# Weight transfers that also wait for the landing of the fourth one ahead

## The chip, the core and the metric

The kernel runs on one core of a Trainium2 chip. The metric is the device time of one execution in microseconds (us); the time before is the median of three runs. The core has a matrix engine (TensorE, PE; its weight loads are listed as PEld), a vector engine (VectorE, DVE), a scalar engine (ScalarE, ACT), GpSimd (POOL) and SyncE (SP). SP computes nothing here: it issues the transfers that bring weights from the chip's main memory to the core. The transfers run on 16 DMA engines, and the landing of a transfer is told to the other engines by a semaphore.

## The reference, cut to what matters

```python
x = A_x
x = x + _A_ref(_layernorm(x), A_mem0, A_Wq, A_Wk, A_Wv, A_Wo, 32)   # attention with a memory
x = x + _B_ref(_layernorm(x), B_w1, B_w2, B_w3, B_w4)               # mixer and MLP
x = x + _A_ref(_layernorm(x), A_mem0, A_Wq, A_Wk, A_Wv, A_Wo, 32)
x = x + _B_ref(_layernorm(x), B_w1, B_w2, B_w3, B_w4)

def _A_ref(x, mem0, Wq, Wk, Wv, Wo, seg_len):     # S = 2048, Dm = 640, 32 heads of 192, M = 8
    mem = mem0
    for s in range(S // seg_len):                 # 64 segments of 32 tokens, one after the other
        h = concatenate([mem, xs], axis=1)        # 40 rows
        q, k, v = h @ Wq, h @ Wk, h @ Wv          # each Wq, Wk, Wv: 640 x 6144
        o = softmax(mask(q @ k.T * scale)) @ v @ Wo
        mem = o[:, :M, :]                         # the next segment's memory
        outs.append(o[:, M:, :])
```

`_B_ref` is a gelu layer of 640 x 640 (`w1`), a shift of quarters of the channels along the tokens, a second layer of 640 x 640 (`w2`), and an MLP 640 to 1536 to 640 (`w3`, `w4`) with layer norms and residuals. All data is bf16. Each segment depends on the memory of the one before, so the 64 segments of an attention layer cannot be run together, and every segment needs all of the attention weights again.

## The kernel before

**Lanes and steps.** The work is cut into 69 steps, one call of `attention_step(t)` each. The first attention layer works on segment t in step t (lane 0), the second one on segment t - 5 (lane 1, `LAG` is 5). Steps 0 to 4 have lane 0 alone, steps 64 to 68 lane 1 alone, and the steps between have both lanes, whose 40 rows each are put side by side as 80 columns. In every second step the mixer and MLP of 64 tokens of each lane are worked in between (`chunk`, `chunk_end`).

**Weights.** They do not all fit on the core. Some stay (`wo` and parts of `wq`, `wk`, `wv`); the rest is brought again in every step. `load_pair` (L802) brings one row block of `Wq`, `Wk` or `Wv` for eight heads, 128 x 1536 values or 384 KB, into one of the 12 buffers of a ring (`wst`, `RING_A`). `load_b` (L838 to L844) brings a piece of `w1` to `w4`, 320 or 160 KB, into one of three buffers (`wstB`, `RING_B`). The projections on TensorE (`keys_queries`, L928, and `values3`, L984) use a block a few microseconds after it has landed. `project` (L1122) multiplies by the `wo` that stays; L1044 makes the scores, L1079 the transposes, L1096 the product with the values.

**Order.** All operations of all steps are handed to a planner (`Plan`) with a cost each, a due time (in steps of 48 us of its own reckoning) and the buffers they use. `place` lays them out in one list, and each engine executes its part in that order. For a weight transfer the planner reckons with a rate and with a lead (`DMA_AHEAD`) over its model of the transfers' line; where this moves a transfer later than its buffer would ask, it is marked `paced`, and the kernel ties it to the TensorE operation that the plan has ended by then:

```python
elif o.paced:
    k = len(done) - 1
    while k >= 0 and done[k].end + PE_LAT > o.start + PACE:
        k -= 1
    if k >= 0:
        tc.add_manual_dep(o.last, done[k].last.name, dep, reason="pace")
```

So SP issues the transfers in the list's order, each after its waits: for TensorE (the pacing, or the last use of the buffer), and for a landing. Eight semaphores tell of the landings of SP's transfers in turn, so a transfer also waits for the landing of the eighth one ahead of it, which used the same semaphore.

Of the kernel before, what the change touches and what calls it, by code (L numbers as in the profile page):

```python
# [20 lines left out]
LAG = 5  # L21
# [4 lines left out]
STEP = 48.0  # L26
# [35 lines left out]
RATE_ONE = 350.0e3  # L62
NSTEPS = 64
LAST_PACE = 0.55


RANK = {
# [517 lines left out]
def kernel(  # L585
# [707 lines left out]
    def chunk(c):  # L1293
        last = c == NCH - 1
        base = (T_A if last else 2 * c + 2) * STEP
        D = lambda x: base + (x * LAST_PACE if last else MIX[0] + x * MIX[1]) * STEP
        plan.at("last" if last else "chunk", base)
# [257 lines left out]
    def chunk_end(c):  # L1555
        last = c == NCH - 1
        base = (T_A if last else 2 * c + 2) * STEP
        D = lambda x: base + (x * LAST_PACE if last else MIX[0] + x * MIX[1]) * STEP
        plan.at("last_end" if last else "chunk_end", base)
# [125 lines left out]
    ctx.enter_context(tc.manual_schedule())  # L1685
    dep = mybir.DependencyInfo(mybir.DependencyClass.Sync, mybir.DependencyReason.DATA)
    done = []
    for o in placed:
        k = len(nc.cur_bb.bb.instructions)
        o.fn(o)  # L1690
        o.last = nc.cur_bb.bb.instructions[-1]
        for x in o.after:
            tc.add_manual_dep(nc.cur_bb.bb.instructions[k], x.last.name, dep, reason="after")
        if o.e == "PE":
            done.append(o)
        elif o.paced:
# [5 lines that stand above are left out]
# [35 lines left out]
```

## Time and profile before

| | us |
|---|---|
| time, median of three runs | 3266.26 (3263.81 to 3273.18) |
| the profiled execution's own time | 3268.68 |
| its span in the profile | 3266.9 |
| TensorE busy (PE) | 3149.0 |
| weight loads busy (PEld) | 2790.2 |
| VectorE / ScalarE / GpSimd busy | 2285.5 / 1854.6 / 269.6 |
| moved by DMA | 833.44 MB, 255 GB/s in the mean |
| granted TensorE clock | 0.993 of full speed |

A profile is one execution. PE and PEld overlap, so their sum means nothing. A row of waits says which engine stood idle before which line, and whose work or whose transfer ended that; "issue" means that no such cause is recorded. A "q" behind an engine's name (SPq) is its sequencer, which only waits and issues. The time "to landing" of a transfer runs from its issue on SP to the last of the 16 signals of its semaphore.

### The profile page before, as it was taken

The numbers are of one execution on the slowest core, as the hardware profiler recorded it, in microseconds if no ns is written. First come the engines' busy times: TensorE is split into PE (matmuls) and PEld (weight loads), VectorE is DVE, ScalarE is ACT, GpSimd is POOL, SyncE is SP. The second block draws the span as 40 slices with busy tenths as digits, with TensorE's granted clock in tenths as the row PEclk, the third lists the DMA queues.
The fourth block names the chain that finished last, engine by engine and source line by source line (L and its number), as shares of the span: only waits on it lengthen the run. The fifth ranks groups of instructions, "written<-read, shape, count | busy, mean of one in ns | idle before, by whom it ended". The sixth has DMA issues, their size and how long they took to land.

```text
span 3266.9 us, 172868 instructions
## 1 busy us (share of the span) xinstructions
PE 3149.0 (96%) x77161; PEld 2790.2 (85%) x77161; DVE 2285.5 (70%) x7377; ACT 1854.6 (57%) x4217; POOL 269.6 (8%) x510
## 2 busy tenths in 40 slices
PE   5899999999999999999999999999999999999997
PEld 4778888888888888888888888888888888888875
DVE  3566777777677777777777777777777777767665
ACT  2345565666556666656565666565656665556443
POOL 0000000000000000000000000000000000000000
PEclk8999999999999999999999999999999999999999
DMA  9787777778777877787777777777877787778885
GB/s 372 264 286 236 237 265 253 241 235 273 246 237 249 280 239 234 253 272 239 245 262 258 241 237 269 253 241 244 281 247 238 244 274 249 238 244 277 275 277 199
DMA packets 409714, 833.44 MB, mean 255 GB/s; under 512 B 39651, under 2 KB 207280, under 8 KB 408969
## 3 DMA queue, kind: packets, MB, share of 16 engines
q1 hardware_dynamic: 401704, 809.47, 73.2%
q0 software_dynamic: 7104, 12.84, 1.3%
q8 instruction: 604, 9.90, 1.2%
q14 instruction: 142, 1.16, 0.1%
q10 hardware_dynamic: 160, 0.08, 0.0%
HBM read 816.98 MB, written 5.24 MB: 252 GB/s over the span
## 4 chain that ended last, share of the span: by engine, by line
PE 88%; DMA 7%; issue 2%; DVE 2%; ACT 1%; SPq 0%; POOL 0%; POOLq 0%; ACTq 0%; DVEq 0%
PE psq L928 16%; PE psy L1122 16%; PE psk L928 16%; PE psv L984 15%; PE pss L1044 5%; PE pso L1096 5%; PE psh L1531 3%; DMA wst<-in_A_Wq_dram 3%; PE y L1577 3%; PE pst L1079 2%; DMA wst<-in_A_Wk_dram 2%; PE psv L1024 2%; PE psh L1409 1%; PE hs L1468 1%; DMA wst<-in_A_Wv_dram 1%
## 5 line engine op out<-in xcount | busy, mean ns | idle before, releaser
L928 PEld LDWEIGHTS <-wst 128*128 128x128 bf16 x19872 | 803.7, 99 | 64.1 <-issue 35.7
L1122 PE MATMUL psy<-oT,wo 128*128 128x80 bf16 (+1 forms) x16560 | 703.6, 200 | 26.4 <-issue 8.6
L964 ACT CAST V<-psv 96x384 bf16<-96x384 f32 (+3 forms) x1264 | 595.9, 474 | 168.3 <-PE psv L984 102.4
L1122 PEld LDWEIGHTS <-wo 128*128 128x128 bf16 x16560 | 630.8, 99 | 51.2 <-issue 35.1
L928 PE MATMUL psq<-hT,wst 128*128 128x80 bf16 (+1 forms) x9936 | 518.0, 200 | 13.7 <-DMA wst<-in_A_Wq_dram 8.6
L928 PE MATMUL psk<-hT,wst 128*128 128x80 bf16 (+1 forms) x9936 | 508.6, 200 | 17.7 <-DVE hT L1149 9.6
L939 ACT CAST qT<-psq 128x480 bf16<-128x480 f32 (+1 forms) x552 | 291.8, 529 | 371.2 <-PE psq L928 352.0
L1104 ACT CAST oT<-pso 128x480 bf16<-128x480 f32 (+1 forms) x552 | 293.7, 532 | 264.0 <-PE pso L1096 238.9
L954 DVE CAST kT<-psk 64x160 bf16<-64x160 f32 (+1 forms) x1104 | 340.4, 308 | 131.3 <-PE psk L928 62.6
L984 PEld LDWEIGHTS <-hT 128*32 128x32 bf16 (+1 forms) x11840 | 295.5, 96 | 157.0 <-issue 5.2
L1063 ACT ACTIVATE Pm<-pss,sm 80x320 bf16<-80x320 f32 (+2 forms) x552 | 279.3, 506 | 195.9 <-DVE sm L1056 105.2
L1056 DVE CUSTOM_DVE_ANT_1 pss<-pss,mask 80x320 f32<-80x320 f32 (+2 forms) x552 | 257.1, 466 | 150.1 <-PE pss L1044 138.3
L1087 ACT COPY PT<-pst 80x320 bf16<-80x320 bf16 (+2 forms) x552 | 221.7, 402 | 239.2 <-PE pst L1079 233.3
L984 PE MATMUL psv<-wst,hT 128*32 128x384 bf16 (+1 forms) x5920 | 343.3, 326 | 2.2 <-issue 1.1
L984 PE MATMUL psv<-wv,hT 128*32 128x384 bf16 x5920 | 344.7, 328 | 0.5 <-issue 0.5
L1067 DVE TENSOR_REDUCE sm<-Pm 80x4 f32<-80x320 bf16 (+2 forms) x552 | 250.5, 454 | 109.6 <-ACT Pm L1063 98.1
L928 PE MATMUL psq<-hT,wq 128*128 128x80 bf16 (+1 forms) x6624 | 321.1, 200 | 4.1 <-DMA wq<-in_A_Wq_dram 2.7
L928 PE MATMUL psk<-hT,wk 128*128 128x80 bf16 (+1 forms) x6624 | 321.0, 200 | 3.4 <-issue 2.0
L928 PEld LDWEIGHTS <-wk 128*128 128x128 bf16 x6624 | 270.8, 99 | 17.6 <-issue 13.9
L947 DVE CAST kT<-psk 128x320 bf16<-128x320 f32 (+1 forms) x552 | 253.8, 460 | 45.6 <-PE psk L928 33.5
L1069 DVE TENSOR_TENSOR Pm<-Pm,sm 80x320 bf16<-80x320 bf16 (+2 forms) x552 | 256.2, 464 | 34.9 <-DVE sm L1068 0.9
L928 PEld LDWEIGHTS <-wq 128*128 128x128 bf16 x6624 | 267.4, 99 | 6.5 <-DMA wq<-in_A_Wq_dram 3.0
(131 smaller groups left out, 3777.6 us busy)
## 6 DMA issues: line engine op xcount, KB each, us to landing
wst<-in_A_Wk_dram SPq DMA_DIRECT2D x556, 384.0 KB, 4.9
wst<-in_A_Wq_dram SPq DMA_DIRECT2D x556, 384.0 KB, 5.0
wst<-in_A_Wv_dram SPq DMA_DIRECT2D x418, 384.0 KB, 5.1
wstB<-in_B_w_dram SPq DMA_DIRECT2D x495, 320.0 KB, 4.7
wstB<-in_B_w_dram SPq DMA_DIRECT2D x132, 160.0 KB, 4.3
wo<-in_A_Wo_dram SPq DMA_DIRECT2D x8, 960.0 KB, 12.3
wv<-in_A_Wv_dram SPq DMA_DIRECT2D x2, 1536.0 KB
xw<-in_A_x_dram POOLq DMA_DIRECT2D x32, 77.5 KB, 5.3
```

Source lines behind the costliest of these rows:

```text
L928: nc.tensor.matmul(out=o[:, cc, 0:W], lhsT=wv(kc, GW * j + cc * P, GW * j + (cc + 1) * P), rhs=h[:, kc, cw:cw + W], start=begin(pq), stop= ...
L939: nc.scalar.copy(out=qT[:, :, c0:c0 + N], in_=T(pq)[:, :, off:off + N])
L947: nc.vector.tensor_copy(out=k4[:, :, 0::3, c0:c0 + N], in_=p4[:, :, 0::2, off:off + N])
L954: copy(out=k4[r0:r1, :, jj, c0:c0 + N], in_=p4[r0:r1, :, 1, off:off + N])
L964: (nc.vector.tensor_copy if e == "DVE" else nc.scalar.copy)(out=v_part(*dst), in_=a_)
L984: nc.tensor.matmul(out=o[32 * u:32 * u + n3, :], lhsT=left[:, kc, 32 * g3:32 * g3 + n3], rhs=wv(kc, a, a + GWH), start=(kc == 0), stop=(kc ...
L1056: nc.vector.tensor_tensor_reduce(out=o, in0=o, in1=maskt.unsqueeze(1).to_broadcast([NR, HG, N]), scale=-scale, scalar=3.0e38, op0=ALU.add, ...
L1063: nc.scalar.activation(out=Pb[0:NR, :, 0:N], in_=o, func=ACT.Exp, bias=sm_[0:NR, 0:1], scale=-1.0)
L1067: nc.vector.tensor_reduce(out=sm_[0:NR, 2:2 + HG], in_=Pb[0:NR, :, 0:N], axis=AX.X, op=ALU.add)
L1069: nc.vector.tensor_tensor(out=Pb[0:NR, :, 0:N], in0=Pb[0:NR, :, 0:N], in1=sm_[0:NR, 6:6 + HG].unsqueeze(2).to_broadcast([NR, HG, N]), op=A ...
L1104: nc.scalar.copy(out=o_[:, :, off:off + N], in_=T(pso)[:, :, 0:N])
L1122: nc.tensor.matmul(out=o[:, m, cw:cw + W], lhsT=wo[:, cc, m * P:(m + 1) * P], rhs=o_[:, cc, 0:W], start=st, stop=True, skip_group_check=True)
```

## The change

In steps with two lanes, which the change takes as those transfers of SP whose due time lies from step 5 to step 63, each transfer is given one more dependence: on the landing of the transfer that stands four places ahead of it among these. The dependence is added as the list is written out, after the planner is done; the plan, the order on every engine, the buffers and the pacing are as before.

```diff
+FLYING = 4
...
     done = []
+    flying = []
     for o in placed:
         k = len(nc.cur_bb.bb.instructions)
         o.fn(o)
         o.last = nc.cur_bb.bb.instructions[-1]
         for x in o.after:
             tc.add_manual_dep(nc.cur_bb.bb.instructions[k], x.last.name, dep, reason="after")
+        if o.e == "SP" and o.dma and LAG * STEP <= o.due < NSTEPS * STEP:
+            flying.append(o)
+            if len(flying) > FLYING:
+                tc.add_manual_dep(o.last, flying[-1 - FLYING].last.name, dep, reason="flying")
         if o.e == "PE":
             done.append(o)
```

## The prediction

> **What bounds the kernel now.** I read the page from the top (busy time, slices, chain), then the waits of TensorE, then the weight queue alone: its issues in order of time, the time to landing, and the busy share of the DMA engines by stretch.
>
> The page, sections 1, 2 and 4:
>
> ```profile
> span 3266.9 us, 172868 instructions
> PE 3149.0 (96%) x77161; PEld 2790.2 (85%) x77161; DVE 2285.5 (70%) x7377; ACT 1854.6 (57%) x4217; POOL 269.6 (8%) x510
> ...
> DMA  9787777778777877787777777777877787778885
> ...
> PE 88%; DMA 7%; issue 2%; DVE 2%; ACT 1%; SPq 0%; POOL 0%; POOLq 0%; ACTq 0%; DVEq 0%
> ```
>
> TensorE works 96% of the span and is 88% of the chain. So whatever delays its weights goes straight into the span, and the most that any change to the weights can win is what TensorE now loses to them. The waits of TensorE in the steps with two lanes (260 to 3070 us; columns: waited for, total us, times, longest us) say how little that is:
>
> ```profile
> PEld L928 <- issue: 37.8, 99, 1.1
> PEld L1044 <- issue: 28.9, 88, 1.2
> PEld L928 <- DMA wst<-in_A_Wq_dram: 10.8, 21, 1.2
> PEld L928 <- DMA wst<-in_A_Wk_dram: 5.7, 12, 0.9
> ```
>
> Waits on weights are 10.8 + 5.7 = 16.5 us of 2810 us, plus about 1 us on `wstB`. "Issue" is a wait for nothing that the profile shows; most are short.
>
> Now the weight queue (SP). First its issues around one burst (start, us, line, count):
>
> ```profile
> 1532.22 1.26 SPq L802 DMA_DIRECT2D wst<-in_A_Wk_dram  x2
> 1534.44 1.27 SPq L802 DMA_DIRECT2D wst<-in_A_Wq_dram  x2
> ...
> 1547.70 2.20 SPq L802 DMA_DIRECT2D wst<-in_A_Wk_dram  x3
> 1551.04 2.26 SPq L802 DMA_DIRECT2D wst<-in_A_Wq_dram  x3
> 1554.17 2.81 SPq L840 DMA_DIRECT2D wstB<-in_B_w_dram  x3
> ```
>
> Second the time from issue to landing (last column) at the burst's first two transfers, and between 1544 and 1558 us:
>
> ```profile
> wst<-in_A_Wk_dram SPq DMA_DIRECT2D x2, 384.0 KB, 3.4
> ...
> wst<-in_A_Wk_dram SPq DMA_DIRECT2D x4, 384.0 KB, 5.7
> wst<-in_A_Wq_dram SPq DMA_DIRECT2D x4, 384.0 KB, 5.6
> ```
>
> Third the stretches of one pair of steps (last columns: clock, DMA share, GB/s):
>
> ```profile
> 1532.00:1544.00 12.00, 12.00 (x306) 10.78 (x303) 9.71 (x33) 7.30 (x17) 2.12 (x3) 1.00 0.86 275
> 1544.00:1558.00 14.00, 14.00 (x341) 12.52 (x339) 10.32 (x33) 9.69 (x21) 0.44 (x2) 1.00 0.95 333
> 1566.00:1580.00 14.00, 13.95 (x348) 12.54 (x345) 9.67 (x32) 9.08 (x21) 0.00 (x0) 1.00 0.39 110
> 1580.00:1596.00 16.00, 16.00 (x389) 14.46 (x389) 12.07 (x37) 9.03 (x20) 0.00 (x0) 1.00 0.96 318
> ```
>
> The weights come in two bursts of some 32 us per pair of steps (94 us), with pauses between. In a burst the DMA engines are 95% busy, a transfer starts about every 1.07 us (28 from 1532.2 to 1562.2, counted in the timeline) and needs 5.6 us to land, against 3.2 to 3.4 us when nothing is ahead of it.
>
> **The change part by part.** Nothing is moved: in the two instruction lists all five engines have the same instructions in the same order. What differs is a wait at 1,857 of the 2,200 transfers on SP. Before, a transfer waits for the TensorE work that it is paced by and for the use of its buffer, and (as the completion semaphores go round in eight) for the landing of the eighth ahead. Now it waits for the fourth ahead. Four terms follow.
>
> (a) SP's own time. The wait is carried by a semaphore instruction that is there already; SP is idle most of the time (its longest total wait is for `psk`, 558.5 us). Cost nothing. GpSimd's and ScalarE's own DMA queues are not held. What stands behind a held transfer is every later weight transfer, for SP issues in order.
>
> (b) How often it holds. At a pace of 1.07 us the fourth ahead was issued 4.3 us earlier and lands after 5.0 us (the median over all `wst`: 4.9 to 5.1 us on the page). So in a burst nearly every transfer is held, by about 0.7 us. Counting issue against landing through the trace from 240 to 3080 us gives the same: 1,021 of 1,903 transfers left before the fourth ahead had landed, by 0.73 us in the mean, 3.2 us at most.
>
> (c) What a held issue does to the landing. The trace has no such wait, so I bound it from both sides.
> Low end: the DMA engines are a line in which each transfer waits for those ahead. At 404 GB/s, the best slices between 1544 and 1558 us, 384 KB (393,216 bytes) take 0.97 us; four of them are 3.9 us of work, and a transfer with nothing ahead lands in 3.2 us. The line then never runs dry, a later issue only waits less in it, and nothing lands later: 0 us. By order of arrival in the trace (landings in a crowded burst follow each other at 0.97 us again and again) this is the nearer end.
> High end: the time to landing stays as it is. Then four in flight allow one transfer per 5.0/4 = 1.26 us with the semaphore's 0.05 us, and a burst of 28 ends 28 x (1.26 - 1.07) = 5 us late. Walking through all transfers so, each with its own old time to landing and TensorE late when the landing is, gives 160 us.
> The Trainium skill would give zero: "DMA: Bandwidth & Descriptors" (Anatomy of one DMA) puts a transfer at a fixed 2.0 us plus its bytes over 436 GB/s, an estimate of 2.9 us here (its fit is for transfers from GpSimd). At 0.97 us each, three in flight would then fill the engines, and a fourth is spare. The trace has 3.2 us for a lone one, near the rule, but 5.6 us in a burst, so I do not take the rule's zero.
> Below zero: the same page (Latency and other measured facts) has HBM access at 0.2 us on average and 2 us at high load, so that a lighter load makes the fixed part smaller. If a shorter line were a lighter load, each landing could come up to 1.8 us sooner, and the 16.5 us of waits on weights would go: -16.5 us. I do not take it: a burst moves the same bytes in the same time (0.95 share), which is the same load, and no row shows a shorter landing at an equal share.
> What I take: the margin in (c) is 3.9 - 3.3 = 0.6 us. A disturbance on a single one of the 16 engines that is longer than this is no longer absorbed, since the landing needs all 16. The page shows one kind: 604 instruction packets with 1.2% of the 16 engines, so 0.012 x 16 x 3266.9 / 604 = 1.04 us each, one every 5.4 us on one engine. Each may cost 1.04 - 0.6 = 0.44 us of lateness in a burst, and there are 2 x 32 / 5.4 = 12 in a pair of steps.
>
> (d) What lateness costs TensorE. Most transfers land long before use (median 4.2 us, counted from landing to the first weight load that waits for it), and there lateness is covered by that slack. 317 of 1,903 (17%) land less than 1 us before use; without cover, one of these costs its whole lateness. 12 x 0.44 x 0.17 = 0.9 us per pair, 26 us over 29.5 pairs; as the slack of these 317 is on average half gone only, I take half: 13 us. It falls at the weight loads of L928, which have the waits now (`psq`, `psk`), first at the ends of the bursts.
>
> Sum: 13 us on 3268.7 us, the profiled execution's own time (span 3266.9). The median shown is 2.4 us lower, so 3266.3 + 13 = 3279 us.
>
> **The rivals.**
> 1. Free (20%): the line drains as at the low end, slack takes the rest. For it: 0.95 DMA share, landings at even distance. Against it: the tight transfers, and the 320 and 160 KB transfers of `wstB`, which make a line of four shorter than 3.9 us. 3266 us, within 5 us.
> 2. Faster (25%): the shorter line lets TensorE's instructions through, which come by the same engines as packets of 16 KB. Place: the long "issue" waits. 17 of them from 250 to 3070 us are over 0.45 us, 15 us together (up to 1.5 us each), and 11 of these begin with five or six weight transfers in flight, a state that holds in under a quarter of the time. The cap removes just those depths. Price: if four fifths of the 15 us go and nothing lands late, -12 us: 3254 us. Against it: the packets themselves last about 1 us at any depth, and six of the 17 waits begin at a depth of four or less. Point of decision: it wins when the lateness of (d) stays under what the instructions gain, so at half the value that I took for (d) and most of the long waits gone.
> 3. Latency-bound (12%): much of the 5.6 us is not line. The high end then counts in part; a third of the 160 us is +53 us: 3319 us. Against it: the 0.97 us distance in crowded bursts.
> 4. My forecast, a partly covered lateness, +5 to +35 us: 43%.
> That the wait does nothing is excluded by (b), unless most transfers had their fourth ahead landed; they had not.
>
> **How the numbers follow.** About 0.3% (10 us) is what a measurement of this kernel can tell from no change. Faster by more: 0.25 less the weak part of rival 2, 0.23. Slower by more: 0.12 from rival 3 and most of 0.43, together 0.53. Within: the rest, 0.24. The range runs from rival 2 at 3254 us to the better end of rival 3 at 3318 us. The likeliest case's own range is 3271 to 3301 us.
>
> **What the changed profile would show.** SP with waits on `DMA wst` hundreds of times, around 0.7 us each, where it has almost none now; time to landing in a burst down from 5.6 towards 4.5 us; DMA share in a burst still over 0.9, or the line has run dry. Right: waits of weight loads at L928 on `wst` up from 16.5 to about 30 us. Wrong upwards: these waits over 60 us, bursts stretched. Wrong downwards: them unchanged or less, with fewer long "issue" waits. If the span changes with neither row, my account is wrong.

## The result, and the profile after

The changed kernel takes 3296.56 us in the median of seven runs (3281.93 to 3306.81), the kernel before, beside it, 3263.81 us (3252.73 to 3273.18). The ratio is 1.0107 with a 95% interval of 1.009 to 1.0124: slower by about 35 us (the two medians differ by 33). The forecast was slower by 13 us.

The profiled execution of the changed kernel took 3281.93 us, the fastest of its seven, so its rows show 13 us of the loss (3281.93 - 3268.68). That this is the forecast's own figure is chance. The lines of its page that answer to those shown of before:

```profile
span 3280.2 us, 172926 instructions
PE 3154.3 (96%) x77161; PEld 2791.8 (85%) x77161; DVE 2283.6 (70%) x7377; ACT 1856.1 (57%) x4217; POOL 268.9 (8%) x510
...
DMA  9787778777777877787778777777877787778785
...
PE 78%; DMA 17%; ACT 2%; DVE 1%; issue 1%; SPq 0%; POOL 0%; POOLq 0%; ACTq 0%; DVEq 0%
```

Busy times and the row of DMA shares are as before; only the chain differs. Weight transfers were 7% of it and are 17%: some 330 us more of chain for 13 us of loss, since a wait for a landing, however short, puts the whole transfer from its issue on into the chain. The waits of TensorE in the same stretch as before (the lines of the kernel have moved by one; L985 is `values3`):

```profile
PEld L929 <- issue: 28.1, 77, 0.6
PEld L929 <- DMA wst<-in_A_Wq_dram: 27.9, 49, 1.8
PEld L1045 <- issue: 27.8, 88, 0.3
PEld L929 <- DMA wst<-in_A_Wk_dram: 8.6, 17, 0.8
PE psv L985 <- DMA wst<-in_A_Wv_dram: 7.7, 11, 1.7
```

Waits for `Wq` blocks have grown from 10.8 to 27.9 us. And SP does now wait for landings, as the change says (columns: waited for, total, times, longest):

```profile
SPq L803 <- PE psk L929: 462.1, 226, 12.5
SPq L803 <- DMA wst<-in_A_Wq_dram: 247.6, 319, 2.4
SPq L803 <- DMA wst<-in_A_Wk_dram: 194.2, 266, 3.2
SPq L803 <- DMA wstB<-in_B_w_dram: 172.9, 253, 2.7
```

The stretch from 1544 to 1558 us, first the DMA share and GB/s in its last columns, then two of its groups of transfers with their time to landing:

```profile
1544.00:1558.00 14.00, 14.00 (x341) 12.52 (x338) 9.55 (x31) 8.62 (x19) 0.43 (x2) 1.00 0.94 308
...
wst<-in_A_Wk_dram SPq DMA_DIRECT2D x4, 384.0 KB, 4.4
wst<-in_A_Wq_dram SPq DMA_DIRECT2D x3, 384.0 KB, 5.4
```

A transfer lands sooner after its issue (4.4 us for 5.7 with `Wk`, 5.4 for 5.6 with `Wq`), yet 308 GB/s move where 333 did, at a DMA share of 0.94 for 0.95. The 28 transfers of this burst, from first issue to last, take 31.6 us for 29.6.

The account closes. Between the same two weight loads near 250 and 3070 us of before, the changed kernel takes 15.1 us more (2835.2 for 2820.1). Idle time before weight loads that a DMA ended went from 16.8 to 37.4 us, idle time of the kind "issue" from 102.4 to 98.1, idle time ended by other engines stayed at 20.0: +20.6 - 4.3 = +16.3 us (gaps over 0.1 us).

The 4.3 us hide two opposite things. One is late `Wv`. In `values3` the block is what the matmul streams, so the matmul waits for it (7.7 us in the last row above, 0.8 us before), and the weight load that stands behind it is listed under "issue" (before, then after):

```profile
PEld L984 <- issue: 5.2, 10, 1.5
...
PEld L985 <- issue: 12.3, 19, 1.9
```

Of the 12.3 us, 10.3 coincide with a matmul that waits for `Wv`; before it was 1.3 us. The other is late instructions, seen in the first row above (28.1 us, longest 0.6; before 37.8, longest 1.1). "Issue" waits over 0.45 us number 17 before and 17 after. Of those before, 11 (11.2 us) end 1.2 to 1.6 us after the end of an instruction packet; of those after, 2 (2.2 us) do, while 11 are the waits at `values3`. (A packet comes every 5.3 us, so that about one wait in thirteen would end so by chance.) In this execution, then, late weights cost 20.6 + 9.0 = 29.6 us, and late instructions gave back about 9.

### The profile page after: what moved, and what is told of

It reads as the page before. It is cut to its first block, busy times and chain, and to the rows that moved or that the text cites. A ratio compares the mean times of both kernels' runs of the same rounds, so it can differ in the third digit from the quotient of the medians.

```text
span 3280.2 us, 172926 instructions
## 1 busy us (share of the span) xinstructions
PE 3154.3 (96%) x77161; PEld 2791.8 (85%) x77161; DVE 2283.6 (70%) x7377; ACT 1856.1 (57%) x4217; POOL 268.9 (8%) x510
## 3 DMA queue, kind: packets, MB, share of 16 engines
q14 instruction: 141, 1.16, 0.1%
## 4 chain that ended last, share of the span: by engine, by line
PE 78%; DMA 17%; ACT 2%; DVE 1%; issue 1%; SPq 0%; POOL 0%; POOLq 0%; ACTq 0%; DVEq 0%
PE psk L929 15%; PE psy L1123 15%; PE psq L929 15%; PE psv L985 13%; DMA wst<-in_A_Wq_dram 7%; DMA wst<-in_A_Wv_dram 4%; PE pso L1097 4%; PE pss L1045 4%; DMA wst<-in_A_Wk_dram 3%; PE psh L1532 3%; PE pst L1080 2%; PE y L1578 2%; PE psv L1025 2%; PE psh L1410 1%; PE hs L1469 1%
## 5 line engine op out<-in xcount | busy, mean ns | idle before, releaser
L929 PEld LDWEIGHTS <-wst 128*128 128x128 bf16 x19872 | 804.0, 99 | 80.2 <-DMA wst<-in_A_Wq_dram 34.6
L929 PE MATMUL psq<-hT,wst 128*128 128x80 bf16 (+1 forms) x9936 | 518.1, 200 | 25.3 <-DMA wst<-in_A_Wq_dram 18.4
L929 PE MATMUL psk<-hT,wst 128*128 128x80 bf16 (+1 forms) x9936 | 509.9, 200 | 19.6 <-DVE hT L1150 9.6
L985 PEld LDWEIGHTS <-hT 128*32 128x32 bf16 (+1 forms) x11840 | 296.5, 96 | 162.4 <-issue 12.3
L985 PE MATMUL psv<-wst,hT 128*32 128x384 bf16 (+1 forms) x5920 | 344.8, 326 | 7.9 <-DMA wst<-in_A_Wv_dram 7.7
L985 PE MATMUL psv<-wv,hT 128*32 128x384 bf16 (+1 forms) x5920 | 344.1, 328 | 0.0
L929 PE MATMUL psq<-hT,wq 128*128 128x80 bf16 (+1 forms) x6624 | 320.7, 200 | 3.0 <-DMA wq<-in_A_Wq_dram 2.4
L929 PE MATMUL psk<-hT,wk 128*128 128x80 bf16 (+1 forms) x6624 | 320.6, 200 | 1.3 <-DVE hT L1155 0.6
L929 PEld LDWEIGHTS <-wk 128*128 128x128 bf16 x6624 | 270.5, 99 | 15.3 <-issue 11.7
L929 PEld LDWEIGHTS <-wq 128*128 128x128 bf16 x6624 | 267.4, 99 | 5.4 <-DMA wq<-in_A_Wq_dram 2.6
```

The costliest lines, as they stand in the source:

```text
L929: nc.tensor.matmul(out=o[:, cc, 0:W], lhsT=wv(kc, GW * j + cc * P, GW * j + (cc + 1) * P), rhs=h[:, kc, cw:cw + W], start=begin(pq), stop= ...
L985: nc.tensor.matmul(out=o[32 * u:32 * u + n3, :], lhsT=left[:, kc, 32 * g3:32 * g3 + n3], rhs=wv(kc, a, a + GWH), start=(kc == 0), stop=(kc ...
```

## The experiments

All but the two that measure the rate alone are made from the changed kernel. Times are against the kernel before, run beside each: ratio, 95% interval.

**The rate alone.** Each stage issues 48 transfers (32 at two in flight, 16 at one) of 384 KB in a row; `ring[n % c]` makes each wait for the landing of the c-th ahead.

```python
for n in range(N[c]):
    kc, col = k % 5, (k // 5) % 4
    nc.sync.dma_start(out=ring[n % c][:], in_=src[:, kc, W * col:W * (col + 1)])
    k += 1
```

`micro_line`:

> Measures the disputed rate alone: 384 KB transfers of Wq in a row on SP into 8 buffers, none of the network is computed (the output is a copy of x); a transfer waits for the landing of the c-th ahead, c = 8, 6, 5, 4, 3, 2, 1 in stages, first with all other engines idle, then (c = 8 to 2) beside a stream of small matmuls whose instructions are fetched meanwhile. Line theory (a lone transfer lands in 3.3 us, the engines need 0.97 us each): quiet stages at 0.97 us per transfer for c = 8 to 4, 1.1 for c = 3, 1.65 for c = 2, 3.3 for c = 1; beside matmuls 0.05 to 0.2 us more at c = 4 and nothing at c = 8. Latency theory (5 us to landing whatever is ahead): 1.2 us or more at c = 4 and 1.6 at c = 3 even in the quiet stages. Instruction packets as the disturbance: the stages beside matmuls differ from the quiet ones at c = 4 and 5 more than at c = 8; if they do not, something else disturbs.

In this run the issues of the later stages were mixed with each other (nothing held the written order), so that only the first three say what was asked: 0.98 us per transfer at c = 8, 6 and 5, and 7.8, 5.9 and 4.9 us to landing. That is a full line: the time to landing is c times 0.98. By the trace, four were in flight for the next 48 transfers, still with idle engines (last columns: clock, DMA share, GB/s), which is 1.16 us per transfer:

```profile
143.30:191.00 47.70, 0.00 (x0) 0.00 (x0) 0.00 (x0) 0.00 (x0) 1.00 0.97 341
```

`micro_line2`, with the written order held:

> The rate alone again, with the order of issue held as written: in the first measurement only the stages with 8, 6 and 5 in flight had it (0.98 us per transfer, 7.8, 5.9 and 4.9 us to landing, so a full line); the later stages were mixed. None of the network is computed; the output is a copy of x. Line theory: 0.98 us per transfer at c = 4 with idle engines too, 3.3/c at c = 3 and below; beside matmuls the line with instruction packets needs 0.05 to 0.2 us more at c = 4, and little at c = 8. Latency theory: 1.2 us at c = 4 with idle engines already. If quiet c = 4 is over 1.05 us, something other than instruction packets breaks the line at four.

Its stages, measured in one execution, each row one of them: c = 6, 5, 4, 3, 2, 1 with idle engines, then c = 8, 5, 4, 3 beside matmuls.

```profile
44.00:93.00 49.00, 0.00 (x0) 0.00 (x0) 0.00 (x0) 0.00 (x0) 1.00 1.03 402
93.00:143.00 50.00, 0.00 (x0) 0.00 (x0) 0.00 (x0) 0.00 (x0) 1.00 1.03 401
143.00:197.00 54.00, 0.00 (x0) 0.00 (x0) 0.00 (x0) 0.00 (x0) 1.00 0.97 339
197.00:261.00 64.00, 0.00 (x0) 0.00 (x0) 0.00 (x0) 0.00 (x0) 1.00 0.91 301
261.00:319.00 58.00, 0.00 (x0) 0.00 (x0) 0.00 (x0) 0.00 (x0) 1.00 0.77 220
319.00:370.00 51.00, 0.00 (x0) 0.00 (x0) 0.00 (x0) 0.00 (x0) 1.00 0.47 129
371.00:422.00 51.00, 41.96 (x1078) 41.35 (x1076) 0.00 (x0) 0.00 (x0) 1.00 0.98 373
509.00:565.00 56.00, 50.60 (x1386) 49.89 (x1384) 0.00 (x0) 0.00 (x0) 1.00 0.94 340
577.00:638.00 61.00, 60.07 (x1671) 59.83 (x1667) 0.00 (x0) 0.00 (x0) 1.00 0.92 313
643.00:715.00 72.00, 71.77 (x2005) 71.67 (x2002) 0.00 (x0) 0.00 (x0) 1.00 0.85 266
```

Counted from landing to landing within each stage, the first eight landings left out:

| in flight | 8 | 6 | 5 | 4 | 3 | 2 | 1 |
|---|---|---|---|---|---|---|---|
| us per transfer, other engines idle | 0.98 | 0.99 | 0.98 | 1.15 | 1.31 | 1.86 | 3.16 |
| us per transfer, beside matmuls | 0.99 | 1.01 | 1.11 | 1.23 | 1.49 | 2.06 | |
| median us to landing, idle | 7.8 | 5.9 | 4.9 | 4.5 | 3.9 | 3.7 | 3.2 |

Both theories miss. The line is full with five in flight and is not with four, even with no other traffic: 1.15 us per transfer where the line theory said 0.98 and the latency theory 1.2, and at three 1.31, between their 1.1 and 1.6. At four, landing takes 4.5 us, more than the 3.9 us of a full line of four and more than the 3.2 us of a lone transfer. The stream of matmuls, with the fetch of its instructions, adds 0.08 us at four, 0.13 at five, 0.01 at eight. And the share misleads: 0.97 at 339 GB/s against 1.03 at 401 GB/s.

**Where the loss is paid: `odd4` and `even4`.**

```diff
-            if len(flying) > FLYING:
+            if len(flying) > FLYING and int(o.due // STEP) % 2 == 1:      # odd4; == 0 in even4
```

> The cap of four only for transfers that are due in odd steps. In the profile after, the new waits of TensorE lie at the end of the burst of the odd steps, where a block is used as it lands, though the transfers of the even steps are later. If it is slack that decides: nearly the whole loss, +25 to +33 us on the kernel before. If lateness itself decides (1.8 us at the end of an even step's burst, 0.6 us in an odd one's): a third or less, +5 to +11 us.

> The cap of four only for transfers that are due in even steps. If slack decides: 0 to +6 us on the kernel before. If lateness itself decides: +20 us or more.

`odd4`: 1.0085 (1.0071 to 1.0098), +28 us. `even4`: 1.0018 (1.0008 to 1.0029), +6 us. Together that is the whole loss, and five sixths of it belong to the odd steps. Yet their lateness is the smaller one. It is counted for each transfer as its landing against the same landing of the kernel before, TensorE's own delay at that time taken off (means by thirds of a burst's transfers, us):

| | odd burst: start, middle, end | even burst: start, middle, end |
|---|---|---|
| cap of four in all steps | 0.0, 0.3, 0.5 | 0.0, 0.6, 1.5 |
| odd steps alone | 0.0, 0.4, 0.4 | none |
| even steps alone | none | 0.0, 0.6, 1.4 |

So slack decides. The waits of `odd4`, in the slowest of its six executions:

```profile
PEld L929 <- DMA wst<-in_A_Wq_dram: 30.3, 48, 1.8
...
PEld L929 <- DMA wst<-in_A_Wk_dram: 9.5, 20, 0.9
```

and of `even4`:

```profile
PEld L929 <- DMA wst<-in_A_Wq_dram: 11.2, 20, 1.3
...
PEld L929 <- DMA wst<-in_A_Wk_dram: 6.2, 14, 1.2
```

The first are near those of the changed kernel (27.9 and 8.6), the second near those of before (10.8 and 5.7).

**Along the burst: `oddlate4`.**

```diff
-            if len(flying) > FLYING:
+            if len(flying) > FLYING and o.due / STEP % 2 >= 1.7:
```

> The cap of four only for the transfers with the last 30% of the due times of an odd step (13 per step, at the end of the burst). If single late landings at the tight end cost the time: nearly all of what the cap in whole odd steps costs, +20 to +28 us. If the lateness builds up along the burst and is paid at its end: less than half, +5 to +12 us.

1.004 (1.0024 to 1.0055), +13 us, lies between the two expectations and decides for neither: the transfers with the last due times of an odd step (12 per step, by the plan) alone make about half of the 28 us. They get about as late by themselves (0.4 us in the last third) as with the whole burst held. `odd4` has 12 us more of waits on weights in its profile; 7 of these fall on the same last transfers and 5 on those of the middle, but it is one execution of each.

**How many in flight: `fly5`, `fly6`, `fly3`.** `FLYING` is 5, 6 or 3.

> A cap of five in all steps with two lanes. Line with disturbances: the margin grows from 0.6 to 5 x 0.97 - 3.3 = 1.6 us, over the 1.04 us of an instruction packet, so 0 to +5 us. Latency-bound at 4.8 us: one transfer per 0.96 us is allowed, under the pace of 1.07 us, so small as well, +5 to +10 us. If the loss is simply in proportion to the holds: about half of the loss at four, +15 us. If fewer transfers in flight help the instruction fetch at all, here it could be faster by up to 10 us.

> A cap of six with the pacing: 203 of 1,903 transfers had five or more ahead of them before the change and would hardly be held. If depth harms the instruction fetch here as it does without pacing: 0 to 8 us faster than the kernel before. If the pacing keeps the line shallow enough: the same within 3 us, as with five.

> A cap of three. The rate measured alone beside matmuls is 1.49 us per 384 KB at three in flight (1.23 at four). A pair of steps moves 24.0 MB (255 GB/s x 94.3 us), as much as 61 such transfers: 91 us at that rate, of the 94 us that the pair takes, and the two bursts can no longer end in time. If the measured rate decides: TensorE waits for wst in both kinds of steps and the time rises by 100 to 300 us. If only a rare late landing decides, as at four: under +70 us.

Five: 0.9992 (0.9982 to 1.0002). Six: 0.9998 (0.9986 to 1.001). Neither can be told from the kernel before. Three: 1.1077 (1.1051 to 1.1103), +351 us, more than the 300 us of the expectation. Its waits in the stretch from 260 to 3070 us alone are

```profile
PEld L929 <- DMA wst<-in_A_Wq_dram: 172.9, 108, 4.9
PEld L929 <- DMA wst<-in_A_Wk_dram: 65.9, 67, 2.8
```

and now the even bursts wait too (half of the DMA waits). Not all of it is waiting: the granted clock fell as well (240 to 3420 us; 1.00 in the same steps before),

```profile
240.00:3420.00 3180.00, 2895.04 (x68141) 2566.87 (x68142) 2044.60 (x6507) 1705.04 (x3772) 239.84 (x446) 0.97 0.71 223
```

in 39 stretches at half of full speed, 208 us together. Between the same two weight loads as above, `fly3` takes 356 us more than before: 251 us of waits on weights, 29 of "issue", and the rest, 76 us, is work that went slower; 208 us at half speed lose up to 104, so these stretches can account for it.

From 0 to 351 us the steps are not even: 6 and 5 cost nothing, 4 costs 35, 3 costs ten times that. This follows the rates measured alone, 1.01, 1.11, 1.23 and 1.49 us per 384 KB beside matmuls. A burst asks for more than four can give: from first issue to last the 28 transfers of 1532 to 1562 us take 29.6 us, and as six of them are short pieces, that is 1.18 us per 384 KB.

**Short pieces: `bytes4`.** The cap counts bytes, 4 x 384 KB.

```diff
-                tc.add_manual_dep(o.last, flying[-1 - FLYING].last.name, dep, reason="flying")
+            left, at = FLYING * 2 * P * PW, len(flying)
+            while at and left >= flying[at - 1].dma:
+                at -= 1
+                left -= flying[at].dma
+            if at:
+                tc.add_manual_dep(o.last, flying[at - 1].last.name, dep, reason="flying")
```

> The cap counts bytes and not transfers: at most four times 384 KB in flight, so that 320 and 160 KB pieces let a fifth one go. The pieces of wstB are a quarter of the transfers, and six of them stand in the burst of an odd step. If the short pieces that count as a full place make the line run dry: a third or more of the loss goes, +10 to +20 us on the kernel before instead of +33. If the line runs dry at four full transfers already, as the rate of 1.15 to 1.23 us measured alone says: little changes, +25 to +33 us.

1.0076 (1.0053 to 1.0099), +25 us. The interval overlaps that of the change, so short pieces that take a full place may be part of the loss, and the runs do not settle how much. Its profile has 52 us of waits on weights in the stretch, more than the changed kernel's 37, but it is the slowest of six executions against the fastest of seven.

**Without pacing: `nopace4`, `nopace8`, `nopace5`.**

```diff
-        elif o.paced:
+        elif o.paced and not (o.e == "SP" and LAG * STEP <= o.due < NSTEPS * STEP):
```

with a cap of four, without a cap (the eight semaphores remain), and with a cap of five.

> The cap of four, and the pacing waits taken from the transfers of the steps with two lanes, so that each goes as soon as its buffer is free and the fourth ahead has landed; the order is the same. If the loss at four is a rate that is too low at a burst's end, starting the burst earlier gives the time back: within 8 us of the same kernel without pacing and without the cap. If four in flight cost at every landing: +20 us and more over that kernel.

> The control for the one before: the pacing waits taken away, no cap beyond the eight semaphores. Transfers go earlier and the line is deeper: up to eight in flight. If depth by itself harms (instruction fetch behind a deep line): slower than the kernel before by 5 to 20 us, with more long issue waits. If the pacing was needed only for slack: 0 to 5 us faster.

> No pacing waits, and a cap of five instead of four. Without pacing, four in flight leave 45 us of waits on weights and few long issue waits (15), eight leave 8 us and 95 long issue waits worth 100 us. Five in flight run at 1.11 us per transfer beside matmuls, near the pace of a burst: waits on weights 10 to 20 us, long issue waits 15 to 40 us. So 3255 to 3285 us; faster than the kernel before only if both stay at the low end. If the loss without pacing comes from the earlier start and not from depth, it stays near the +31 us of the cap of four or the +98 us of no cap.

`nopace4`: 1.0095 (1.0077 to 1.0113), +31 us. `nopace8`: 1.0299 (1.028 to 1.0319), +98 us. `nopace5`: 1.0045 (1.0034 to 1.0056), +15 us. The comparison of the first two came out the other way round from both expectations, since `nopace8` is by far the slowest. Its waits say why:

```profile
PEld L929 <- issue: 94.6, 152, 2.3
...
PE psq L929 <- issue: 30.1, 30, 2.2
...
PEld L929 <- DMA wst<-in_A_Wk_dram: 3.4, 9, 0.7
```

Weights are hardly late any more (8 us of waits); TensorE waits for "issue". Of these waits 95 are longer than 0.45 us (17 before), 101 us together (15 before). In 91 of the 95 TensorE resumes 1.2 to 1.6 us after the end of an instruction packet, in 76 of these of one that came 6 us or more after the last one: it had run out of instructions. With five in flight the weights are in time too (1.6 us of waits), and 35 long "issue" waits with 27 us are left, 34 of them of this kind. With four, 15 with 10 us (7 of this kind), but 45 us of waits on weights. Whether an earlier start gives time back at four was not tested by this: the odd burst starts within 0.1 us of where it started before, in `nopace8` too, so the pacing is not what holds its start. Its landings are as late as with pacing (0.0, 0.4, 0.4 us along it).

The stretch's accounts: `odd4` +23.9 us of DMA and +3.6 us of issue for +25.0 us of length; `nopace8` -8.8 and +89.0 for +85.2.

No version that was run beats the kernel before.

## Why the prediction was wrong in size

**Right.** The sign; that the order and all else stay, and that the wait holds: 1,021 transfers had left before the fourth ahead had landed, 29 do now. The place: `psq` and `psk` at L929 at the ends of the bursts, though `Wv` at L985 was left out. That SP's own time costs nothing: `fly5` has waits of the same kind in its program and loses nothing. Time to landing in the crowded stretch fell as forecast for `Wk` (4.4 us) and not for `Wq` (5.4 us).

**Step (c), the margin: wrong.** It let only an instruction packet do harm, as four in flight were to leave 0.6 us to spare. The rate alone shows no margin at four: 1.15 us per transfer with nothing else running, 1.23 beside matmuls. The pace to hold this against is not the 1.07 us of the prediction, which divides by 28 where 28 issues have 27 distances (29.6/27 = 1.10) and takes short pieces for full ones; per 384 KB it is 1.18. So the line runs dry a little in every burst, and lateness adds up along it: over all transfers of a pair of steps it is 29 us in the profile (7.6 odd, 21.4 even), where 12 packets at 0.44 us made 5.3. What misled was the 0.95 DMA share read as a full line: a full line is 1.03 and 401 GB/s, and the 333 GB/s of the burst stood beside the 0.95. Instruction packets may be a part (matmuls add 0.08 us per transfer at four), but not the cause.

**The rule of the skill** (the Trainium skill, "DMA: Bandwidth & Descriptors", Anatomy of one DMA): the estimate of 2.9 us from its fit is near the 3.16 us measured for a lone transfer. Dividing it by 0.97 to get the number in flight that fills the engines (three) fails: it takes five. The measurement decides.

**Step (d), the cover: wrong in form.** It made a lateness cost 0.17 x 0.5 = 8.5% of itself, a mean over two kinds of bursts. `odd4` and `even4` show that they differ fivefold in cost, the later landings being the cheaper ones. The tight loads stand together at the end of the odd bursts, and there a delay of half a microsecond is paid; in the even bursts three times as much is covered. In the profile 29.6 us are paid over 29.5 pairs, 1.0 us per pair where I had 0.44: lateness over five times as large, of which only 3.4% is paid. The two errors partly cancel, so that even the order of size owes something to luck. In the median time it is 33/29.5 = 1.1 us.

**Rival 2** was real, though it did not win. Its place was right: of the 11 long waits that end after an instruction packet the cap left 2, 11.2 us down to 2.2, which is 9 of the 12 us that it promised. What it lacked was that late weights cost three times as much. Such long waits number 6 or 7 in the other profiles with the cap of four in all or in even steps (`bytes4`, `nopace4`, `even4`), and 9 to 19 in `odd4`, `oddlate4`, `fly5` and `fly6`; each is one execution, so the gain is known roughly only. At full depth without pacing the same waits grow to 96 us (`nopace8`). **Rival 1** (free) is what a cap of five does. **Rival 3** (latency-bound, +53 us) had the better rate and too little cover. The test that I named for the line, a DMA share over 0.9, could not have told: it reads 0.94 in the slower burst.

**Left open.** Why four transfers do not fill the line with idle engines. A landing needs the last of 16 signals, and from the first to the last of them it is 0.5 us in the median for a lone transfer and 1.4 us with four in flight; but it is 1.4 us with five as well, where the line is full, so this spread alone does not explain it, and no run takes it away. And the profiled execution of the change lost 13 us where the median lost 33: the rows of the slower executions are not seen.

## What to carry to other kernels

Measure the rate at a given number of transfers in flight by itself before you cap it: here 384 KB transfers need five with idle engines and six beside matmuls (1.01 us per transfer for 1.11), and the cost rises from nothing at five to 1% at four and 11% at three (about a fifth of the last is a lower granted clock). Read how full the DMA engines are from GB/s against the best GB/s seen, not from their busy share. And look for the loads with no slack: lateness elsewhere, even three times as large, cost almost nothing. An "issue" wait is not one thing: look at what else ends beside it before you count it as unchanged.

## What the runs showed of the hardware that was not expected

- 384 KB transfers in a row on one queue: 129, 220, 301, 339, 401 GB/s with 1, 2, 3, 4, 5 in flight, and no more with 6 (402 GB/s) or 8 (0.98 us per transfer for 0.98).
- Too deep a line has a price as well: with up to eight in flight and no pacing, TensorE lost 96 us to long waits that end just after an instruction packet, though hardly a weight was late; a cap of four in the paced kernel took such waits from 11.2 to 2.2 us.
- The busy share of the DMA engines falls only from 1.03 to 0.91 while the bytes moved fall by a quarter (401 to 301 GB/s).
